# Gated attention and a maxout layer on one core: the product of the scores with v as seven half-block products in place of eight

## The chip, the core and the metric

The kernel runs on one core of a Trainium2 chip. Its time is the device time of one execution in microseconds, the median of several runs. TensorE (PE in the profile) does matrix products into PSUM, VectorE (DVE) and ScalarE (ACT) do elementwise work, GpSimd (POOL) issues the loads, and SyncE (SP) issues the transposing DMAs and the stores.

## What is computed

Eight sequences of 3072 rows. For each, with z of width 64 and u, v of width 256:

```python
scores = scale * np.matmul(z, z.transpose(0, 2, 1))     # scale = 1/3072
attn = np.maximum(scores, 0.0) ** 2
x = u * np.matmul(attn, v)                              # 24576 x 256 over all sequences
h1, h2 = x @ w1, x @ w2                                 # width 1024
out = np.maximum(h1, h2) @ w_out                        # 24576 x 256, float32
```

The kernel works in bfloat16 with float32 sums. It uses max(h1, h2) = relu(x (w1 - w2)) + h2, so that the second half of the layer is g w_out + x (w2 w_out), where the 256x256 product w2 w_out (`W2o_sb`) is made once.

## The kernel before

**Blocks.** A sequence is 24 blocks of 128 rows, and four blocks are a group, so there are six groups. One *step* makes one group of 512 output rows of the attention: 48 steps in all, `steps[n]` with `n = 6 b + s`. A step needs the squared scores of all 24 key blocks against its 512 rows.

**Scores.** z z^T is symmetric, so only the blocks on and above the diagonal are made (`scores_pair` for two key blocks by 512 rows, `scores_diag` for a group against itself). TensorE writes a pair into a PSUM tile of two banks (`s_ps`), ScalarE takes the relu into SBUF (`r_sb`, L218), VectorE squares it (`a_sb`, L221). Blocks above the diagonal are also turned by a transposing DMA into `aT` tiles, which a later step reads. The groups that a step reads turned are its `early` groups, the others are its own. Only in the first sequence are the first four groups made in both forms without turning.

**Products with v.** For each key block k and each half dc of v's columns, `attn` gives one matmul: 128x128 of v as weights, 128x512 of squared scores as the moving operand, summed in PSUM over the 24 blocks in `xacc0` and `xacc1`, one bank each. That is 48 matmuls of 512 columns per step. `epilogue` (L268) multiplies by u and scale on VectorE and gives `xT`.

**The layer.** `chunk_d` makes x (w1 - w2) in four pieces of 4 matmuls of 512 columns; each piece's relu goes to ScalarE or VectorE, whichever the scheduler finds free (`nc.any`, L292). `chunk_o` makes the output in two pieces of 20 matmuls of 256 columns, copied by ScalarE (L323) and stored.

**Order.** All matmuls, loads and SP's DMAs are pinned to program order. A list `work` holds the pieces of TensorE's work with a planned duration: products, d pieces (864 ns), o pieces (2180 ns). Steps are staggered, so that the d and o pieces of steps two and three back (`LAG = 3`) lie between the products of this step. Scores are made in *windows* of up to three pairs, which are laid into `work` from the last to the first, each as late as its rows are due (`LAT_OWN` and the like before use) and at least `GAP` apart, and not close to a d or o piece. VectorE's and ScalarE's instructions are placed by the scheduler by priority; `high_priority` puts some ahead. PSUM has eight banks: three tiles of two banks (`mm_psum`) are shared by scores, d and o pieces, two banks hold the sums of the products.

Of the kernel before, what the change touches and what calls it, by code (L numbers as in the profile page):

```python
# [11 lines left out]
def kernel(  # L12
# [31 lines left out]
    GW = G * P  # L44
    NG = NSB // G
# [5 lines left out]
    NA, NT, ND = 18, 12, 3  # L51
# [6 lines left out]
    vpool = ctx.enter_context(tc.tile_pool(name="vpool", bufs=2))  # L58
    ulpool = ctx.enter_context(tc.tile_pool(name="ulpool", bufs=3))
    upool = ctx.enter_context(tc.tile_pool(name="upool", bufs=3))  # L60
    xpool = ctx.enter_context(tc.tile_pool(name="xpool", bufs=LAG + 2))
    apool = ctx.enter_context(tc.tile_pool(name="apool", bufs=NA))
    dpool = ctx.enter_context(tc.tile_pool(name="dpool", bufs=ND))
    tpool = ctx.enter_context(tc.tile_pool(name="tpool", bufs=NT))
    gpool = ctx.enter_context(tc.tile_pool(name="gpool", bufs=2))
# [5 lines left out]
    pin = tc.keep_in_program_order  # L71

# [30 lines left out]
    def new_v():  # L103
        return vpool.tile([P, NSB, D], bf16, name="v_sb")

    def load_v(b, v_sb, t0, n):
        load(
            out=v_sb[:, ds(t0, n), :],
            in_=v[b].rearrange("(p t) d -> p t d", p=P)[:, ds(t0, n), :],
        )  # L110
# [40 lines left out]
    for q in seqs:  # L151
        q.T = {}
        q.u_sb = {}
        q.uT = {}

    w1_sb = consts.tile([P, KD, Dff], bf16)
    w2_sb = consts.tile([P, KD, Dff], bf16)
    w_out_sb = consts.tile([P, KF, D], bf16)
    w2T_sb = consts.tile([P, KD, KF, P], bf16)
    W2o_sb = consts.tile([P, KD, D], bf16)  # L160

    def subtract_weights():
        pin(nc.vector.tensor_sub(w1_sb, w1_sb, w2_sb))

    def turn_w2():
        sp_dma(
            out=w2T_sb.rearrange("p c n q -> p (c n) q"),
            in_=w2_sb.rearrange("p c f -> p (c f)"),
            transpose=True,
        )  # L170

    def fold_w2o():
        for dc in range(KD):
            w2o_ps = mm_psum.tile([P, D], fp32, name="w2o_ps", tag="mm")
            for nb in range(KF):
                matmul(
                    w2o_ps,
                    w2T_sb[:, dc, nb, :],
                    w_out_sb[:, nb, :],
                    start=(nb == 0),  # L180
                    stop=(nb == KF - 1),
                )
            nc.any.tensor_copy(W2o_sb[:, dc, :], w2o_ps)

# [17 lines left out]


    def scores_pair(b, s, k0):
        q = seqs[b]
# [4 lines left out]
        a_sb = apool.tile([P, 2, GW], bf16, name="a_sb")  # L210
        r_sb = apool.tile([P, 2, GW], bf16, name="r_sb", bufs=3)

        head = b == 0 and s == 0 and k0 < 12
        keep = pin if head else lambda ins: None
        if head and k0 in (2, 10):
            keep(nc.vector.tensor_single_scalar(out=r_sb, in_=s_ps, scalar=0.0, op=ALU.max))
        else:
            keep(nc.scalar.activation(r_sb, s_ps, AF.Relu))  # L218
        if head:
            yield  # L220
        keep(nc.vector.tensor_mul(a_sb, r_sb, r_sb))  # L221
        gj = k0 // G
        if gj > s and not direct(b, s, gj):
            if (s, gj) not in q.T:
                q.T[s, gj] = tpool.tile([P, G, G, P], bf16, name="aT")
            turn(
                q.T[s, gj][:, ds(k0 - G * gj, 2), :, :].rearrange("p k q x -> p (k q) x"),
                a_sb.rearrange("p j q -> p (j q)"),
            )
        yield a_sb  # L230
# [3 lines left out]
    def scores_diag(b, s):  # L234
        q = seqs[b]
        k = G * s
        s_ps = mm_psum.tile([P, 2 * G, P], fp32, name="s_ps", tag="mm")
        s2_ps = mm_psum.tile([P, 2 * G, P], fp32, name="s2_ps", tag="mm")
        score(q, s_ps[:, 0:4, :], 0, k, s, 0, 4)
        score(q, s_ps[:, 4:7, :], 1, k + 1, s, 1, 3)  # L240
        score(q, s2_ps[:, 2:4, :], 1, k + 2, s, 2, 2)
        score(q, s2_ps[:, 4:5, :], 0, k + 3, s, 3, 1)
        yield
        aD = dpool.tile([P, G, G, P], bf16, name="aD")
        r_sb = apool.tile([P, 7, P], bf16, name="r_sb", bufs=3)
        nc.scalar.activation(r_sb, s_ps[:, 0:7, :], AF.Relu)  # L246
        r2_sb = apool.tile([P, 3, P], bf16, name="r2_sb", bufs=2)
        nc.vector.tensor_single_scalar(out=r2_sb, in_=s2_ps[:, 2:5, :], scalar=0.0, op=ALU.max)  # L248
        nc.vector.tensor_mul(aD[:, 0, :, :], r_sb[:, 0:4, :], r_sb[:, 0:4, :])
        nc.vector.tensor_mul(aD[:, 1, 1:4, :], r_sb[:, 4:7, :], r_sb[:, 4:7, :])  # L250
        nc.vector.tensor_mul(aD[:, 2, 2:4, :], r2_sb[:, 0:2, :], r2_sb[:, 0:2, :])
        nc.vector.tensor_mul(aD[:, 3, 3, :], r2_sb[:, 2, :], r2_sb[:, 2, :])
        for r in range(G - 1):
            turn(
                aD[:, r + 1 : G, r, :],
                aD[:, r, r + 1 : G, :].rearrange("p q x -> p (q x)"),
            )
        yield aD

    def attn(q, k, moving, xacc, dcs, first, last):  # L260
        for dc in dcs:
            matmul(xacc[dc], q.v[:, k, ts(dc, P)], moving, start=first, stop=last)

    def epilogue(q, s, xacc):
        xT = xpool.tile([P, KD, GW], bf16, name="xT")
        with tc.high_priority(offset=2000):
            for dc in range(KD):
                nc.vector.scalar_tensor_tensor(  # L268
                    out=xT[:, dc, :].rearrange("p (t q) -> p t q", q=P),
                    in0=xacc[dc].rearrange("p (t q) -> p t q", q=P),  # L270
                    scalar=c2,
                    in1=q.uT[s][:, :, dc, :],
# [6 lines left out]
    def chunk_d(xT, g_out):  # L279
        g_sb = gpool.tile([P, KF, GW], bf16, name="g_sb")  # L280
        for nb in range(0, KF, 2):
            d_ps = mm_psum.tile([P, 2, GW], fp32, name="d_ps", tag="mm")
            for j in range(2):
                for kc in range(KD):
# [3 lines left out]
                        xT[:, kc, :],  # L288
# [3 lines left out]
            nc.any.tensor_single_scalar(  # L292
                out=g_sb[:, nb : nb + 2, :], in_=d_ps, scalar=0.0, op=ALU.max
            )
# [5 lines left out]
    def chunk_o(b, c, xT, g_sb, split=False):  # L300
        o_sb = opool.tile([P, G, D], fp32, name="o_sb")
        out_b = out[ds(b * S, S), :].rearrange("(p t) d -> p t d", p=P)
        def block(o_ps, t):
            for nb in range(KF):
                matmul(o_ps, g_sb[:, nb, ts(t, P)], w_out_sb[:, nb, :], start=(nb == 0), stop=False)
            for dc in range(KD):
                matmul(
                    o_ps, xT[:, dc, ts(t, P)], W2o_sb[:, dc, :], start=False, stop=(dc == KD - 1)
                )

        for th in range(G // 2):
# [7 lines left out]
            else:  # L319
# [3 lines left out]
                nc.any.tensor_copy(o_sb[:, ds(2 * th, 2), :], o_ps[:, :, :D])  # L323
# [8 lines left out]
    blank = consts.tile([P, GW], bf16)  # L332
# [12 lines left out]
    q.v = new_v()  # L345
    for t0 in range(0, NSB, G):
        load_v(0, q.v, t0, G)
# [6 lines left out]
    class Step:  # L354
        def __init__(self, b, s):
            self.b, self.s, self.q = b, s, seqs[b]
            self.xacc = None
            self.n = [0] * KD
# [7 lines left out]
            self.scored = {}  # L366

        def begin(self):


            self.xacc = [
                acc_psum.tile([P, GW], fp32, name=f"xacc{dc}") for dc in range(KD)
            ]

        def add(self, k, moving, dcs=range(KD)):
            n = self.n[dcs[0]]
            for dc in dcs:
                self.n[dc] += 1
            attn(self.q, k, moving, self.xacc, dcs, n == 0, n == NSB - 1)

        def add_early(self, k):
            i, qb = divmod(k, G)
            self.add(k, self.q.T[i, self.s][:, :, qb, :])

        def add_own(self, k, dcs=range(KD)):
            self.add(k, self.scored[k - k % 2][:, k % 2, :], dcs)
# [5 lines left out]
        def add_diag(self, j):  # L392
            self.add(G * self.s + j, self.scored[None][:, j, :, :])

        def finish(self):
            assert self.n == [NSB] * KD
            self.xT = epilogue(self.q, self.s, self.xacc)
            fresh[0] = self.xT[:, 0, 0:1]
# [14 lines left out]

    steps = [Step(b, s) for b in range(B) for s in range(NG)]

# [4 lines left out]
    LAT_OWN, LAT_TURNED, LAT_DIAG = 2900, 9000, 10000  # L420
# [3 lines left out]

    def put_early(st, ks):
# [274 lines left out]
```

## Time and profile before

| | |
|---|---|
| time, 3 runs | 981.18, 981.86, 981.88 us; median 981.86 |
| span of the profiled execution (its own time is known only as this span) | 979.7 us |
| TensorE busy, granted clock | 968.9 us (99%), 1.00 |
| VectorE busy | 432.0 us (44%) |
| ScalarE busy | 442.4 us (45%) |
| mean busy share of the DMA engines, by queue | 61.3% (hardware), 21.5% (software) |

The span is the time from the first to the last instruction; the time of a run is some 2 us more. "L74" is line 74 of the kernel; all matmuls have that line, so they are told apart by their tiles. A matmul's duration in the profile includes the time in the array's pipeline; what a stream of them costs is the distance between their starts. The same holds, with a smaller overlap, for VectorE and ScalarE.

### The profile page before, as it was taken

What the parts mean: (1) busy time and instruction counts of PE and PEld (TensorE: products, weight loads), DVE (VectorE), ACT (ScalarE), POOL (GpSimd) and SP (SyncE); (2) the same over time, 40 slices, a digit from 0 to 9 for tenths busy, and PEclk for the clock granted to TensorE, in tenths of its full rate; (3) what the DMA queues carried; (4) which work ended last, traced back from release to release, by engine and by line L of the source; (5) the groups of instructions that cost most, each with busy time, mean ns of one, the idle gap of its engine ahead of it and who ended that gap; (6) DMA issues with size and microseconds to landing.
All of it is one profiled execution on the core that took longest, in us unless ns stands there. A gap on an engine that the chain in (4) does not pass through costs nothing.

```text
span 979.7 us, 14514 instructions
## 1 busy us (share of the span) xinstructions
PE 968.9 (99%) x5661; PEld 510.6 (52%) x5742; DVE 432.0 (44%) x681; ACT 442.4 (45%) x500; POOL 77.5 (8%) x228
## 2 busy tenths in 40 slices
PE   9999999999999999999999999999999999999998
PEld 3355545555455554555545564455545555445556
DVE  6654444443544435433445334444345443554322
ACT  6853454334643355433554335533355433654322
POOL 2011100110001100010000100011000110000000
PEclk9999999999999999999999999999999999999999
DMA  9988899986989979898788968789777896896521
GB/s 150 186 142 150 145 180 153 165 147 114 182 161 149 150 118 180 152 168 130 150 157 144 175 122 164 142 153 181 135 147 149 135 188 126 148 164 115 109 66 65
DMA packets 378517, 143.46 MB, mean 146 GB/s; under 512 B 356944, under 2 KB 358608, under 8 KB 378448
## 3 DMA queue, kind: packets, MB, share of 16 engines
q1 hardware_dynamic: 361888, 112.78, 61.3%
q0 software_dynamic: 16560, 29.74, 21.5%
q8 instruction: 45, 0.74, 0.3%
q14 instruction: 24, 0.20, 0.1%
HBM read 59.77 MB, written 25.17 MB: 87 GB/s over the span
## 4 chain that ended last, share of the span: by engine, by line
PE 99%; issue 1%; DMA 0%; DVE 0%
PE xacc L74 52%; PE o_ps L74 21%; PE d_ps L74 17%; PE s_ps L74 8%; DMA o_sb<-in_z_dram 0%; PE tpz L134 0%; PE w2o_ps L74 0%; DVE o_sb L317 0%; DVE z_sb L343 0%
## 5 line engine op out<-in xcount | busy, mean ns | idle before, releaser
L74 PEld LDWEIGHTS <-v_sb 128*128 128x128 bf16 x2304 | 216.0, 98 | 277.4 <-issue 40.5
L218 ACT ACTIVATE r_sb<-s_ps 128x1024 bf16<-128x1024 f32 x258 | 248.5, 1023 | 111.4 <-PE s_ps L74 111.4
L221 DVE TENSOR_TENSOR a_sb<-r_sb 128x1024 bf16<-128x1024 bf16 x260 | 179.3, 691 | 212.1 <-ACT r_sb L218 207.9
L74 PE MATMUL xacc<-a_sb,v_sb 128*128 128x512 bf16 x997 | 231.0, 379 | 2.3 <-issue 0.2
L74 PE MATMUL xacc<-aT,v_sb 128*128 128x512 bf16 x912 | 216.5, 379 | 0.0
L74 PE MATMUL o_ps<-w_out_sb,g_sb 128*128 128x256 bf16 x1536 | 199.1, 273 | 0.0
L74 PE MATMUL d_ps<-xT,w_sb 128*128 128x512 bf16 x751 | 172.7, 379 | 0.9
L74 PEld LDWEIGHTS <-g_sb 128*128 128x128 bf16 x1536 | 149.9, 98 | 27.6
L292 ACT ACTIVATE g_sb<-d_ps 128x1024 bf16<-128x1024 f32 x96 | 98.3, 1024 | 138.8 <-PE d_ps L74 138.8
L292 DVE TENSOR_SCALAR g_sb<-d_ps 128x1024 bf16<-128x1024 f32 x96 | 117.4, 1223 | 84.7 <-PE d_ps L74 81.3
L323 ACT COPY o_sb<-o_ps 128x512 f32<-128x512 f32 x94 | 55.1, 586 | 178.2 <-PE o_ps L74 178.2
L268 DVE SCALAR_TENSOR_TENSOR xT<-xacc,uT 128x512 bf16<-128x512 f32 x96 | 62.0, 683 | 137.4 <-PE xacc L74 137.4
L74 PEld LDWEIGHTS <-w_sb 128*128 128x128 bf16 x768 | 75.1, 98 | 88.7
L74 PE MATMUL s_ps<-zT 64*128 64x512 bf16 (+3 forms) x696 | 89.2, 359 | 0.1
L246 ACT ACTIVATE r_sb<-s_ps 128x896 bf16<-128x896 f32 x44 | 40.3, 917 | 97.9 <-PE s_ps L74 97.9
L74 PE MATMUL xacc<-aD,v_sb 128*128 128x512 bf16 x331 | 79.9, 379 | 2.6 <-issue 2.2
L74 PE MATMUL o_ps<-W2o_sb,xT 128*128 128x256 bf16 x384 | 73.3, 273 | 0.0
L248 DVE TENSOR_SCALAR r_sb<-s_ps 128x384 bf16<-128x384 f32 x44 | 24.5, 558 | 95.3 <-PE s_ps L74 95.3
L74 PEld LDWEIGHTS <-zT 64*128 64x128 bf16 x696 | 27.2, 94 | 62.2 <-issue 50.4
L83 POOL COPY gate_sb<-g_sb 128x1 bf16<-128x1 bf16 x44 | 8.3, 188 | 420.0 <-DVE g_sb L292 253.2
L74 PEld LDWEIGHTS <-xT 128*128 128x128 bf16 x384 | 37.6, 98 | 4.4
L83 POOL COPY gate_sb<-a_sb 128x1 bf16<-128x1 bf16 x48 | 9.7, 203 | 273.9 <-DVE a_sb L221 273.9
(37 smaller groups left out, 144.2 us busy)
## 6 DMA issues: line engine op xcount, KB each, us to landing
out_dram<-o_sb SPq DMA_DIRECT2D x47, 512.0 KB, 3.7
v_sb<-in_v_dram POOLq DMA_DIRECT2D x48, 256.0 KB, 5.7
u_sb<-in_u_dram POOLq DMA_DIRECT2D x48, 256.0 KB, 5.3
aT<-a_sb SPq DMA_TRANSPOSE x228, 3.7
z_sb<-in_z_dram POOLq DMA_DIRECT2D x7, 384.0 KB, 7.5
aD<-aD SPq DMA_TRANSPOSE x132, 2.4
w_sb<-in_moe_w_dram POOLq DMA_DIRECT2D x2, 512.0 KB, 6.5
uT<-u_sb SPq DMA_TRANSPOSE x48, 4.8
```

Of the source, the lines that this page charges most:

```text
L74: pin(nc.tensor.matmul(*args, **kw))
L83: pin(nc.gpsimd.tensor_copy(gate_sb, tile_ap))
L218: keep(nc.scalar.activation(r_sb, s_ps, AF.Relu))
L221: keep(nc.vector.tensor_mul(a_sb, r_sb, r_sb))
L246: nc.scalar.activation(r_sb, s_ps[:, 0:7, :], AF.Relu)
L248: nc.vector.tensor_single_scalar(out=r2_sb, in_=s2_ps[:, 2:5, :], scalar=0.0, op=ALU.max)
L268: nc.vector.scalar_tensor_tensor(out=xT[:, dc, :].rearrange("p (t q) -> p t q", q=P), in0=xacc[dc].rearrange("p (t q) -> p t q", q=P), sca ...
L292: nc.any.tensor_single_scalar(out=g_sb[:, nb : nb + 2, :], in_=d_ps, scalar=0.0, op=ALU.max)
L323: nc.any.tensor_copy(o_sb[:, ds(2 * th, 2), :], o_ps[:, :, :D])
```

## The change

The products of a step from n = 4 on (`PLAIN = 4`; 44 of 48 steps) are made by a seven-product scheme of the Strassen kind. A product of a 2x2 arrangement of half blocks (two key blocks by two halves of v's columns, with two halves of 256 rows) takes seven matmuls of 256 columns in place of eight. They come in two phases:

- Phase 0: three products for each pair of key blocks, with *sums* of score half blocks (`make_sums`, two VectorE additions per group, into a buffer `es`) as moving operands, and sums of blocks of v (`lf`) as weights. Their three accumulators are copied to SBUF (`finish_sums`: one ScalarE copy of 768 columns, two VectorE additions).
- Phase 1: four products for each pair with score blocks as they are or with differences made in place (`make_split`, two VectorE subtractions per group). `finish` copies all four accumulators to SBUF on ScalarE and combines and scales them on VectorE (three float32 operations of 512 columns, four products with u of 256 columns).

The sums of v are made once per sequence and group (`fold_v`, five VectorE operations). The relus of the d pieces and the copies of the o pieces all go to ScalarE; so do four of five squares of the steps from n = 4 on (`square`). The squares are in place, so `r_sb` is gone. The diagonal group is made as a full pair and a lower quarter: two relus on ScalarE, two squares on VectorE, two turning DMAs in place of three. Phase 0 follows the o pieces of step n - 3; the d pieces of step n - 2 lie between the phases. Buffers: v and the score tiles are held by groups, `ulpool` 2 for 3, `xpool` 4 for 5, `gpool` 1 for 2; the two accumulators are one tile.

The core of the diff ("..." marks what is left out):

```diff
+    PLAIN = 4
-    NA, NT, ND = 18, 12, 3
+    NA, NT = 12, 12
+    vpool = ctx.enter_context(tc.tile_pool(name="vpool", bufs=10))
+    spool = ctx.enter_context(tc.tile_pool(name="spool", bufs=4))
+    epool = ctx.enter_context(tc.tile_pool(name="epool", bufs=1))
+    gpool = ctx.enter_context(tc.tile_pool(name="gpool", bufs=1))
...
+    def soon():
+        return tc.high_priority(offset=2000)
...
+    def fold_v(b, g):
+        q = seqs[b]
+        m = q.v[g].rearrange("p (m k) (c d) -> p m k c d", k=2, c=2)
+        lf = q.lf[g] = lpool.tile([P, 3, G // 2, P], bf16, name="lf")
+        sub, add = nc.vector.tensor_sub, nc.vector.tensor_add
+        add(lf[:, 0], m[:, :, 0, 0, :], m[:, :, 1, 1, :])
+        sub(lf[:, 1], m[:, :, 0, 1, :], m[:, :, 0, 0, :])
+        sub(lf[:, 2], m[:, :, 1, 0, :], m[:, :, 1, 1, :])
+        add(m[:, :, 0, 1, :], m[:, :, 0, 1, :], m[:, :, 1, 1, :])
+        add(m[:, :, 1, 0, :], m[:, :, 1, 0, :], m[:, :, 0, 0, :])
...
+    def square(ap):
+        n_squares[0] += 1
+        if n_squares[0] % 5:
+            nc.scalar.activation(ap, ap, AF.Square)
+        else:
+            nc.vector.tensor_mul(ap, ap, ap)
...
-            nc.any.tensor_single_scalar(
-                out=g_sb[:, nb : nb + 2, :], in_=d_ps, scalar=0.0, op=ALU.max
-            )
+            with soon():
+                nc.scalar.activation(g_sb[:, nb : nb + 2, :], d_ps, AF.Relu)
...
+        def make_sums(self, g):
+            es = spool.tile([P, 3 * GW], bf16, name="es")
...
+                a = self.A[g]
+                rows = es[:, : 2 * GW].rearrange("p (r x) -> p r x", x=HW)
+                nc.vector.tensor_add(rows, a[:, :, 0:HW], a[:, :, HW:GW])
+                cross = es[:, 2 * GW :].rearrange("p (m x) -> p m x", x=HW)
+                t = a.rearrange("p (m k) x -> p m k x", k=2)
+                nc.vector.tensor_add(cross, t[:, :, 0, 0:HW], t[:, :, 1, HW:GW])
...
+        def make_split(self, g):
...
+            nc.vector.tensor_sub(l1, l1, l0)
+            nc.vector.tensor_sub(h0, h0, h1)
...
+        def products(self, g, m, which):
...
+            if which == 0:
...
+                todo = [
+                    (0, lf[:, 2, m, :], rows[:, 2 * m + 1]),
+                    (1, lf[:, 1, m, :], rows[:, 2 * m]),
+                    (2, lf[:, 0, m, :], cross[:, m]),
+                ]
+            else:
+                todo = [
+                    (0, vk[:, 1, ts(1, P)], part[:, 1, 0]),
+                    (1, vk[:, 1, ts(0, P)], part[:, 1, 1]),
+                    (2, vk[:, 0, ts(1, P)], part[:, 0, 0]),
+                    (3, vk[:, 0, ts(0, P)], part[:, 0, 1]),
+                ]
...
+        def finish_sums(self):
+            e = epool.tile([P, 4, HW], fp32, name="e")
...
+                nc.scalar.copy(
+                    e[:, 0:3, :], self.acc.rearrange("p c (h x) -> p (c h) x", h=2)[:, 0:3, :]
+                )
+                self.w = epool.tile([P, 2, HW], fp32, name="w")
+                for h in range(2):
+                    nc.vector.tensor_add(self.w[:, h, :], e[:, h, :], e[:, 2, :])
...
+                nc.scalar.copy(e, self.acc.rearrange("p c (h x) -> p (c h) x", h=2))
+                nc.vector.tensor_add(t1, e[:, 0:2, :], e[:, 2:4, :])
+                nc.vector.tensor_add(w, w, e[:, 0:4:3, :])
+                nc.vector.tensor_sub(w, w, e[:, 1:3, :])
+                for h in range(2):
+                    for dc in range(KD):
+                        nc.vector.scalar_tensor_tensor(
...
-    LAT_OWN, LAT_TURNED, LAT_DIAG = 2900, 9000, 10000
+    LAT_OWN, LAT_TURNED, LAT_DIAG = 6500, 11500, 11500
+    AHEAD = 4500
...
+        if not st.plain:
+            put_o(n - LAG)
+            for which, ns in ((0, 327), (1, 437)):
+                if which:
+                    put(0, False, st.finish_sums)
+                    put_d(n - LAG + 1)
+                put(0, False, st.begin, () if which else "begin")
+                for g in st.groups:
+                    jobs.append((len(work), st, g, which))
...
-    for n in range(last - LAG + 2, last + 1):
-        put_d(n)
-        put_o(n - 1, False)
-    put_o(last, True)
+    put_o(last - LAG + 1)
+    for n in range(last - LAG + 2, last + 1):
+        put_d(n)
+        put_o(n, n == last)
...
-    GAP_FIRST, GAP = 2100, 2500
+    GAP_FIRST, GAP = 2100, 2400
...
-                v_at = [(3, 2), (3, 8), (3, 14), (4, 2), (4, 8), (4, 14)]
+                v_at = [(3, 8), (4, 2), (4, 8), (4, 13), (5, 9.5), (5, 11)]
...
+    waiting = sorted((begins[i] - AHEAD, i, st.n, g, which) for i, st, g, which in jobs)
...
+            elif which:
+                st.make_split(g)
+            else:
+                st.make_sums(g)
```

Sums and differences of a group are put into the program 4500 ns (`AHEAD`, by the planned durations) before the products that read them.

## The prediction

> **What bounds the kernel now.** First the page's busy times and its chain of waits:
>
> ```profile
> PE 968.9 (99%) x5661; PEld 510.6 (52%) x5742; DVE 432.0 (44%) x681; ACT 442.4 (45%) x500; POOL 77.5 (8%) x228
> PE 99%; issue 1%; DMA 0%; DVE 0%
> PE xacc L74 52%; PE o_ps L74 21%; PE d_ps L74 17%; PE s_ps L74 8%; DMA o_sb<-in_z_dram 0%; PE tpz L134 0%; PE w2o_ps L74 0%; DVE o_sb L317 0%; DVE z_sb L343 0%
> ```
>
> The chain is TensorE from end to end, and half of it is products with v. The table of waits shows 2.4 us for matmuls of the products and less for the others. So work taken from TensorE shortens the kernel, as long as the two engines at 45% can carry what is added. Then the groups by shape, for the price of one of each:
>
> ```profile
> L221 DVE TENSOR_TENSOR a_sb<-r_sb 128x1024 bf16<-128x1024 bf16 x260 | 179.3, 691 | 212.1 <-ACT r_sb L218 207.9 <-DMA aD<-aD 0.2
> L292 DVE TENSOR_SCALAR g_sb<-d_ps 128x1024 bf16<-128x1024 f32 x96 | 117.4, 1223 | 84.7 <-PE d_ps L74 81.3 <-issue 0.7
> L292 ACT ACTIVATE g_sb<-d_ps 128x1024 bf16<-128x1024 f32 x96 | 98.3, 1024 | 138.8 <-PE d_ps L74 138.8
> L268 DVE SCALAR_TENSOR_TENSOR xT<-xacc,uT 128x512 bf16<-128x512 f32 x96 | 62.0, 683 | 137.4 <-PE xacc L74 137.4
> L323 ACT COPY o_sb<-o_ps 128x512 f32<-128x512 f32 x94 | 55.1, 586 | 178.2 <-PE o_ps L74 178.2
> L251 DVE TENSOR_TENSOR aD<-r_sb 128x256 bf16<-128x256 bf16 x44 | 12.8, 291 | 1.5
> ```
>
> The figure after the busy time is the mean duration in ns. Durations overlap, so the timeline gives the spacing (start, length, and how many in the piece):
>
> ```profile
> 400.30 1.90 PE L74 MATMUL xacc<-aT,v_sb 128*128 128x512 bf16 x8
> 402.03 1.04 PE L74 MATMUL o_ps<-w_out_sb,g_sb 128*128 128x256 bf16 x8
> ```
>
> ```profile
> 399.88 2.85 ACT L218 ACTIVATE r_sb<-s_ps 128x1024 bf16<-128x1024 f32 x3 [1.03 <-PE s_ps L74]
> 413.92 0.43 DVE L249 TENSOR_TENSOR aD<-r_sb 128x512 bf16<-128x512 bf16 x1
> 414.26 0.35 DVE L250 TENSOR_TENSOR aD<-r_sb 128x384 bf16<-128x384 bf16 x1
> 414.83 0.69 DVE L221 TENSOR_TENSOR a_sb<-r_sb 128x1024 bf16<-128x1024 bf16 x1
> 415.44 1.28 DVE L268 SCALAR_TENSOR_TENSOR xT<-xacc,uT 128x512 bf16<-128x512 f32 x2
> ```
>
> A 512-column matmul costs (1.90 - 0.38)/7 = 0.216 us, one of 256 columns with weights of its own (1.04 - 0.27)/7 = 0.109. ScalarE: (2.85 - 1.02)/2 = 0.91 for 1024 columns. VectorE: 0.61 for a bf16 pair operation of 1024 columns, 0.34 for 512, 0.60 for 512 float32 columns. Each is about 0.09 to 0.11 below its duration.
>
> **TensorE, part by part.** Removed in 44 steps: 48 x 0.216 = 10.37 us. Added: six groups x two pairs of blocks x seven matmuls = 84 x 0.109 = 9.16. The o piece is the witness for 84: small matmuls, each with a new weight load, back to back. Gain 44 x 1.21 = 53.3 us. Turned tiles as moving operands come in four pieces of 128 columns today and cost no more than the others. The diagonal's scores grow from 10 blocks to 12; two 64-row matmuls run beside each other, so it is half a 256-column matmul, some 0.05 us x 44 = 2.2 us. One accumulator tile for two: in the plain steps 1 to 3 the next products wait for both L268 instructions (0.68 each) where now the first half's is over early, 3 x 0.9 = 2.7 us. The last o pieces now stand directly behind their own d pieces and wait for the last relu (about 0.5 us, twice): 1 us.
>
> A full step on TensorE is then 9.16 + d 16 x 0.216 = 3.46 + o 40 x 0.109 = 4.36 + scores 1.6 (8% of the span over 48 steps) = 18.6 us.
>
> **ScalarE per step.** 212 pairs fall into 44 steps, 4.82 each. Relus 4.82 x 0.91 = 4.4; squares 0.8 x 4.82 = 3.86, and no row shows a square there: between 0.91 (this relu) and 1.04 (its whole duration), I take 0.94, since a cast of 256 columns from SBUF (L344, 405 ns) is 0.03 over a copy of 256 from PSUM (L317, 372); 3.6. Diagonal 0.91 + 0.48 = 1.4. Accumulator copies 0.70 + 0.91 = 1.6. All d relus 4 x 0.91 = 3.6, o copies 2 x 0.48 = 1.0. Sum 15.6 us of 18.6, 84%.
>
> By the Trainium skill's page "ScalarE: Activation LUTs", Rules for kernel authors, relus and products belong on VectorE. The trace disagrees for the relus out of PSUM (1024 ns against VectorE's 1223) and bears it out for squares (0.61 on VectorE); with all squares back there VectorE's sum below would be 18.6 us per step, TensorE's own figure, and the forecast would go towards rival 1.
>
> **VectorE per step.** Sums 6 x (0.61 + 0.34) = 5.7; differences 6 x 2 x 0.34 = 4.1; `finish_sums` 2 x 0.34 = 0.7; `finish` 3 x 0.60 + 4 x 0.33 = 3.1; diagonal squares 0.61 + 0.34 = 0.95; its fifth of the squares 0.6; `fold_v` 5 x 0.21 = 1.05. Sum 16.2 us, 87%. From the other side, with whole durations (41 instructions x 0.09 more) it is 19.9. I take 16.2: the rows above overlap even where each follows the other at once.
>
> **Waits.** All of this is off the path only while it comes in time.
> - Between the phases TensorE has the d pieces (3.46) and after phase 1 the o pieces (4.36), ScalarE needs 0.70 and 0.91 for the accumulators: hidden, unless ScalarE is 2.5 us late.
> - d pieces come every 0.86 us and leave ScalarE every 0.91, with three PSUM tiles. If a score window stands right behind them, its third pair waits some 0.2 us for a tile.
> - Sums for phase 0: `finish` holds VectorE for 3.1 us out of the 8.2 us of o pieces and phase 0, in which the six sums need 5.7. That doesn't fit by 0.6, but four `es` buffers let VectorE make the first sums before, out of the 13% that it is free. What can't be made before are rows scored late. The tightest window of own rows stands 1.75 us before phase 1's end (the planner keeps 1.7 us to the next o piece). Three relus, the accumulator copy, the rest of the window before and three squares end about 8.6 us later, the sum at 9.6; TensorE gets there at 1.75 + 0.87 (scores) + 4.36 + four groups x 0.65 = 9.6. So about 0, and 0.3 for the diagonal behind it.
> - Loads: `v_at` puts the last two of a sequence behind the last reader of an old group; POOL's queue waits there, the u load behind it too, and a `fold_v` that VectorE has in its order can hold up everything on it, 0 to 2 us at seven seams; 4 us in all.
>
> I take 0.3 us per step, 13 us, with bounds of 0 and 0.8 (35 us). SP has fewer DMAs (88 diagonal turns for 132), the other turns are the same.
>
> **Sum.** Against the span: 979.7 - 53.3 + 2.2 + 2.7 + 1 + 13 + 4 = 949.3. The median of the runs is 2.2 over the span: 951.5, say 951. Without any wait 979.7 - 53.3 + 2.2 + 2.2 = 930.8; with 35 us of waits and 14 at the seams 983.
>
> **Rivals.**
> 1. *VectorE becomes the bound* (slower). Place: sums, differences and `finish` on one in-order queue. If nothing overlaps, 19.9 us per step: 44 x 1.3 = 57 us over TensorE's floor of 935 (the sum without waits at steps and seams), 992. It decides from 19.8 us per step on (53.3 - 5.9 = 47.4 us to lose, 1.1 per step). For: 87% with two queues that wait for each other, and stretches where ScalarE has three windows in a step. Against: the overlaps. Chance 0.26.
> 2. *Strided operands lose the double rate* (slower). No bf16 pair operation of the trace has pieces of 128 or 256 columns with gaps. If these ran at a column per cycle (L292 on VectorE, 1.14 spacing), sums and differences would be 17.6 instead of 9.8, VectorE 24 us per step, some 1170 us. The Trainium skill, "VectorE: DVE Perf Modes", Mode 2×_1P, asks for 16-bit data of step 1 only, which these have; the trace shows that rate on whole tiles (691 ns). Chance 0.04.
> 3. *Relu and square don't share a table* (slower). The one table load in the trace takes 1.28 us; two per window, 2.3 windows per step, make 5.9 us more on ScalarE: 21.5 per step, about 1065. The Trainium skill, "ScalarE: Activation LUTs", Table sets, names relu and copy as in every set, not square. Chance 0.03.
> 4. *The transfers come too late*: turned tiles and v with the DMA engines at 83% already. Turns take 3.7 us to land and are planned 11.5 ahead; a delay of 1.2 us per step would take the gain. About 990. Chance 0.05.
>
> **Numbers.** TensorE stays the bound: 0.62, its own range 931 to 983. Rival 1 reaches from 970 to 1010 and has a little of "faster". A measurement here tells about 0.2% (2 us) from no change. Faster 0.66, same 0.03, slower 0.31. The range leaves out rivals 2 and 3 and the top of 1: 931 to 1008.
>
> **What would show it.** TensorE's busy time near 920 us; 256-column products 0.109 apart; VectorE and ScalarE each some 740 us of spacing (more in durations); TensorE's waits named `es` (sums), not `acc`. Wrong it is if products wait for VectorE over 1.1 us per step, if small matmuls are over 0.115 apart, or if bf16 sums of 1024 columns take more than 0.7 us.

## The result, and the profile after

The changed kernel takes 1108.28 us (median of four runs, 1104.19 to 1109.73), the kernel before 981.56 beside it: a ratio of 1.1286, 95% interval 1.1265 to 1.1306. It is 12.9% slower; the forecast was 951, faster. The profiled execution took 1108.47 us, with a span of 1106.7 and a mean granted clock of 0.951 (1.000 before).

Busy times, granted clock in 40 slices, and chain, from the page of the changed kernel:

```profile
PE 990.1 (89%) x7326; PEld 678.2 (61%) x7326; DVE 763.8 (69%) x1887; ACT 779.0 (70%) x898; POOL 221.6 (20%) x228
...
PEclk8889978999899998999989999899998999989999
...
PE 47%; ACT 20%; DMA 14%; DVE 11%; issue 7%; POOL 1%; SPq 0%; DVEq 0%; ACTq 0%; POOLq 0%
PE acc L81 24%; PE o_ps L81 10%; PE d_ps L81 9%; DMA v_sb<-in_v_dram 7%; ACT g_sb L323 7%; ACT a_sb L249 6%; DMA aT<-a_sb 6%; ACT a_sb L230 4%; PE s_ps L81 4%; DVE es L462 2%; DVE xT L544 1%; DVE a_sb L253 1%; ACT a_sb L284 1%; ACT e L519 1%; DVE es L465 1%
```

No engine is busy over 89%, and the chain, TensorE from end to end before, is less than half TensorE. Two transfers stand in it: the load of v (7%) and the turning DMAs (6%). From the sixth slice on the clock dips every five slices, about once per sequence. The groups (busy time, mean ns of one; behind the second bar the idle time ahead of them and what ended it):

```profile
L81 PE MATMUL acc<-es,lf 128*128 128x256 bf16 x1584 | 217.7, 286 | 87.7 <-DVE lf L203 52.6
...
L230 ACT ACTIVATE a_sb<-a_sb 128x1024 bf16<-128x1024 bf16 x170 | 183.6, 1102 | 0.9
...
L90 POOL COPY gate_sb<-g_sb 128x1 bf16<-128x1 bf16 x43 | 60.5, 1408 | 487.3 <-ACT g_sb L323 487.3
L462 DVE TENSOR_TENSOR es<-a_sb 128x1024 bf16<-128x1024 bf16 x150 | 102.9, 686 | 39.1 <-ACT a_sb L230 35.3
...
L483 DVE TENSOR_TENSOR a_sb<-a_sb 128x512 bf16<-128x512 bf16 x150 | 63.0, 420 | 61.0 <-DMA aT<-a_sb 60.9
...
L201 DVE TENSOR_TENSOR lf<-v_sb 128x256 bf16<-128x256 bf16 x48 | 13.8, 288 | 104.3 <-DMA v_sb<-in_v_dram 104.3
```

The instructions cost what the forecast said: sums of 1024 columns 686 ns, pieces with gaps 420 ns for 512, squares on ScalarE 1102 ns, and 256-column products 0.110 us apart where nothing holds them (the first line of the timeline below: (2.79 - 0.27)/23). What is new stands behind the second bar: VectorE is idle 104.3 us ahead of the first fold of v and 60.9 us ahead of the differences, and the seven-product matmuls of phase 0 (`acc<-es,lf`) stand 87.7 us. The waits say the same by pairs (us in total, times, longest):

```profile
DVE lf L201 <- DMA v_sb<-in_v_dram: 104.3, 24, 5.9
...
DVE a_sb L483 <- DMA aT<-a_sb: 60.9, 35, 4.0
...
PE acc L81 <- DVE lf L203: 52.6, 15, 9.0
...
ACT e L519 <- DVE a_sb L484: 45.5, 9, 6.6
...
PE acc L81 <- DVE es L462: 34.5, 26, 3.5
PE acc L81 <- DVE xT L298: 10.6, 3, 4.0
```

VectorE waits for v at three or four places of each sequence; one of them lies at the seam, where one sequence goes over into the next, and there TensorE stops too. One seam in the timeline (start, length; in brackets the idle time before and its releaser), from TensorE's, GpSimd's and VectorE's rows:

```profile
414.43 2.79 PE L81 MATMUL acc<-aT,v_sb 128*128 128x256 bf16 x24
...
423.93 3.33 POOL L90 COPY gate_sb<-a_sb 128x1 bf16<-128x1 bf16 x1 [11.45 <-ACT a_sb L230]
427.20 0.53 POOL L93 DMA_DIRECT2D v_sb<-in_v_dram  x1
...
426.53 0.68 DVE L462 TENSOR_TENSOR es<-a_sb 128x1024 bf16<-128x1024 bf16 x1
431.77 0.29 DVE L201 TENSOR_TENSOR lf<-v_sb 128x256 bf16<-128x256 bf16 x1 [4.56 <-DMA v_sb<-in_v_dram]
...
432.79 0.42 DVE L465 TENSOR_TENSOR es<-a_sb 128x512 bf16<-128x512 bf16 x1
...
432.53 1.46 PE L81 MATMUL acc<-es,lf 128*128 128x256 bf16 x6 [5.41 <-DVE lf L203]
434.81 2.74 PE L81 MATMUL acc<-es,lf 128*128 128x256 bf16 x12 [0.82 <-DVE lf L203]
```

Four things are to be seen. The load of v is issued at 427.20, behind a one-column copy of GpSimd (`gate`, which holds a load until a given tile is written) that took 3.33 us; it ended when VectorE's gapless stream of two-input instructions ended (426.53 + 0.68). Before, such a copy took 0.2 us (from the groups of before):

```profile
L83 POOL COPY gate_sb<-a_sb 128x1 bf16<-128x1 bf16 x48 | 9.7, 203 | 273.9 <-DVE a_sb L221 273.9
```

The fold that needs this load is VectorE's next instruction: everything behind it on that queue stands for 4.56 us, among it a score sum (L465) whose blocks were there, since the sum at 426.53 reads the same ones. TensorE then stands 5.41 us. And when it goes on, twelve small matmuls take 2.74 us, 0.22 us each where they took 0.11: half clock.

Adding up the distances between the starts of matmuls, less the usual distance of their kind, TensorE's standstills of over 0.3 us are 131.6 us in 88 places (7.3 us before): 57.5 inside phase 0, 38.9 at the seven seams (4.4 to 6.8 each, between a score window and phase 0). The granted clock is 0.5 in 16 stretches, some 109 us together.

### The profile page after: what moved, and what is told of

It reads as the page before. It is cut to its first block, busy times and chain, and to the rows that moved or that the text cites. A ratio compares the mean times of both kernels' runs of the same rounds, so it can differ in the third digit from the quotient of the medians.

```text
span 1106.7 us, 19307 instructions
## 1 busy us (share of the span) xinstructions
PE 990.1 (89%) x7326; PEld 678.2 (61%) x7326; DVE 763.8 (69%) x1887; ACT 779.0 (70%) x898; POOL 221.6 (20%) x228
## 4 chain that ended last, share of the span: by engine, by line
PE 47%; ACT 20%; DMA 14%; DVE 11%; issue 7%; POOL 1%; SPq 0%; DVEq 0%; ACTq 0%; POOLq 0%
PE acc L81 24%; PE o_ps L81 10%; PE d_ps L81 9%; DMA v_sb<-in_v_dram 7%; ACT g_sb L323 7%; ACT a_sb L249 6%; DMA aT<-a_sb 6%; ACT a_sb L230 4%; PE s_ps L81 4%; DVE es L462 2%; DVE xT L544 1%; DVE a_sb L253 1%; ACT a_sb L284 1%; ACT e L519 1%; DVE es L465 1%
## 5 line engine op out<-in xcount | busy, mean ns | idle before, releaser
L81 PE MATMUL acc<-es,lf 128*128 128x256 bf16 x1584 | 217.7, 286 | 87.7 <-DVE lf L203 52.6
L249 ACT ACTIVATE a_sb<-s_ps 128x1024 bf16<-128x1024 f32 x258 | 251.0, 1039 | 56.8 <-PE s_ps L81 56.3
L81 PEld LDWEIGHTS <-lf 128*128 128x128 bf16 x1584 | 159.0, 102 | 139.3 <-DVE lf L203 60.1
L81 PE MATMUL acc<-a_sb,v_sb 128*128 128x256 bf16 (+1 forms) x1392 | 195.9, 293 | 10.6 <-DVE xT L298 10.6
L323 ACT ACTIVATE g_sb<-d_ps 128x1024 bf16<-128x1024 f32 x192 | 181.8, 1033 | 16.2 <-PE d_ps L81 14.2
L230 ACT ACTIVATE a_sb<-a_sb 128x1024 bf16<-128x1024 bf16 x170 | 183.6, 1102 | 0.9
L90 POOL COPY gate_sb<-g_sb 128x1 bf16<-128x1 bf16 x43 | 60.5, 1408 | 487.3 <-ACT g_sb L323 487.3
L462 DVE TENSOR_TENSOR es<-a_sb 128x1024 bf16<-128x1024 bf16 x150 | 102.9, 686 | 39.1 <-ACT a_sb L230 35.3
L81 PE MATMUL acc<-aT,v_sb 128*128 128x256 bf16 x912 | 111.7, 273 | 0.0
L81 PE MATMUL s_ps<-zT 64*128 64x512 bf16 (+1 forms) x696 | 101.4, 374 | 9.2 <-ACT g_sb L323 2.2
L483 DVE TENSOR_TENSOR a_sb<-a_sb 128x512 bf16<-128x512 bf16 x150 | 63.0, 420 | 61.0 <-DMA aT<-a_sb 60.9
L452 DVE TENSOR_TENSOR es<-aT 128x1024 bf16<-128x1024 bf16 x114 | 78.1, 685 | 12.0 <-DMA aT<-a_sb 10.8
L201 DVE TENSOR_TENSOR lf<-v_sb 128x256 bf16<-128x256 bf16 x48 | 13.8, 288 | 104.3 <-DMA v_sb<-in_v_dram 104.3
L90 POOL COPY gate_sb<-a_sb 128x1 bf16<-128x1 bf16 x41 | 44.2, 1078 | 207.4 <-ACT a_sb L230 143.6
```

The source lines that it names most:

```text
L81: pin(nc.tensor.matmul(*args, **kw))
L90: pin(nc.gpsimd.tensor_copy(gate_sb, tile_ap))
L201: add(lf[:, 0], m[:, :, 0, 0, :], m[:, :, 1, 1, :])
L230: nc.scalar.activation(ap, ap, AF.Square)
L249: keep(nc.scalar.activation(a_sb, s_ps, AF.Relu))
L323: nc.scalar.activation(g_sb[:, nb : nb + 2, :], d_ps, AF.Relu)
```

## The experiments

Four explanations: **v**, the loads of v and the folds behind them hold up VectorE's queue at the seams; **turns**, the differences are made in place and must wait until the turning DMA has read the tile; **amount**, VectorE (rival 1) or ScalarE has too much to do; **clock**, the standstills cost more than their length, since TensorE is slower behind them. The ratios are to the kernel before on the same chip, with 95% intervals. `e2` to `e5`, `e10` and `e11` leave work out and so don't compute the whole result; the others do.

**One cause taken away at a time.**

`e1_no_gate`: `- if is_load:` becomes `+ if is_load and begins[i] < start_of[0, 4]:` ahead of `gate(...)`, so that loads after the first steps aren't held by GpSimd copies.

> The loads from the fifth step of the first sequence on have no GpSimd copy ahead of them any more; they wait only for their buffers. Theory A (the sums of v stand in VectorE's queue and wait for v; v is late because the copy ahead of each load reads SBUF and waits for a gap in VectorE's stream, 1.1 to 4.2 us in the mean in place of 0.2): VectorE's wait for v falls from 104 us to under 40, the time from 1108 to 1030 to 1060. Theory B (v is late because its buffer comes free late): the wait stays over 80 us, time over 1090. Theory C (VectorE simply has too much to do, rival 1 of the prediction): time within 1% of 1108.

1104.19 us, 1.1251 [1.1201, 1.1302]. The time is the one named for **amount** and not the one named for the copies (theory A). But the waits moved: VectorE's wait for v fell from 104.3 to 48.5 us, and its wait for turns rose from 60.9:

```profile
DVE a_sb L483 <- DMA aT<-a_sb: 117.8, 43, 7.6
```

What the loads gave back, the next DMA on the same queue took.

`e2_v_once`: the loads and folds of later sequences are left out, and the first sequence's v serves for all. In their place stands

```diff
+            seqs[c].v, seqs[c].lf = seqs[0].v, seqs[0].lf
```

> v and its sums are loaded and made once and used for all sequences (leaves out the other seven sequences' v and its sums). Theory A: all waits of TensorE for sums of v (7 gaps, 39 us) and VectorE's 104 us for v go, with them some of the gaps for score sums and of the half-clock stretches: 1010 to 1040. Theory C: only the work counts, 1.05 us per step of VectorE: 1060 to 1108. If differences waiting for the turning DMAs were most of it (theory D): over 1070.

1022.95 us, 1.0424 [1.039, 1.0457]: 85 us less, though the 210 folds left out are, at 0.21 us, only 44 us of VectorE, and v's loads are DMAs. The clock rose to 0.985. The wait for turns was now 102.5 us.

`e3_no_war`: the differences of groups that are not read turned go to a tile of their own that nothing reads, so that VectorE does the same work and need not wait for the turning DMA.

```diff
-            nc.vector.tensor_sub(l1, l1, l0)
-            nc.vector.tensor_sub(h0, h0, h1)
+            if g in self.early:
...
+            else:
+                d = spool.tile([P, 3 * GW], bf16, name="es")
+                for i, (x, y) in enumerate(((l1, l0), (h0, h1))):
...
```

> The differences of a step's own groups go to a scratch tile that nothing reads, so that VectorE does the same work but need not wait until the turning DMA has read the scores (leaves out those differences). Theory D (this wait, 61 us of VectorE's idle time, holds up the score sums behind it): 1040 to 1075. Theory A alone: 1095 to 1108. Theory C: within 1% of 1108.

1069.27 us, 1.0896 [1.0864, 1.0927]: 39 us less, with the same arithmetic. v's wait stayed at 101.0.

`e4_no_sums`: no sums and no differences at all, the same number of matmuls on raw blocks.

> No score sums and no differences: the products read the score blocks as they are (leaves out make_sums and make_split, 9.8 us of VectorE per step; the same 84 matmuls). The floor of the prediction is 935. If waits for VectorE are the whole loss: 940 to 985, the rest being the wait for sums of v at seven places (39 us and its clock). If ScalarE can't keep up with relus and squares: over 1020, with TensorE waiting for ScalarE.

1016.44 us, 1.0357 [1.0285, 1.0429], between the two ranges. 92 us of the loss go, and with the differences the wait for turns goes too, so this alone does not tell amount from turns. But **amount** can't be all: VectorE is busy only 342 us, and the kernel is still slower than before, with 138.1 us of VectorE's waits for v. The GpSimd copies are short again here:

```profile
L90 POOL COPY gate_sb<-g_sb 128x1 bf16<-128x1 bf16 x43 | 8.5, 197 | 482.8 <-ACT g_sb L323 464.6 <-DMA a_sb<-a_sb 18.2
```

So the length of the copies isn't what makes v late, or not alone: with short ones, too, a fold stands on VectorE until its load has landed (at one seam a load issued at 381.78 us lands at 388.2, and VectorE waits 5.8 us for it).

`e5_v_once_no_war`: `e2` and `e3` together.

> Both earlier edits together: v and its sums once for all sequences, and own groups' differences into a scratch tile (leaves both out). Theory A+D (the two DMA waits in VectorE's queue, with the half-clock stretches that they cause, are the loss): the single gains were 85 and 39 us of 1108, so 975 to 990, and the granted clock over 0.99. Theory C (VectorE's amount of work): not under 1010.

988.44 us, 1.0076 [1.0048, 1.0103], clock 0.993. Its busy line:

```profile
PE 951.2 (97%) x7326; PEld 669.5 (68%) x7326; DVE 720.3 (73%) x1677; ACT 777.2 (79%) x898; POOL 237.6 (24%) x144
```

VectorE carries 94% of the changed kernel's work and ScalarE all of it, and 120 of the 127 us of loss are gone. The two waits for DMAs, with what hangs on them, were the loss, not the sums; **amount** is out as its cause.

**Order by hand.** The scheduler is free to place VectorE's instructions. It puts some ahead of their plan: in the trace after, score sums of step 4 stand in the plain steps and wait 4.58 us for a turn there, ahead of an `epilogue`.

`e6_pinned`: folds, sums and differences all held in program order (`pin(...)` around each). `e7_pinned_early_v`: also v loaded earlier:

```diff
-    NA, NT = 12, 12
+    NA, NT = 11, 12
...
-    vpool = ctx.enter_context(tc.tile_pool(name="vpool", bufs=10))
+    vpool = ctx.enter_context(tc.tile_pool(name="vpool", bufs=12))
...
-                v_at = [(3, 8), (4, 2), (4, 8), (4, 13), (5, 9.5), (5, 11)]
+                v_at = [(3, 8), (4, 2), (4, 8), (4, 13), (5, 1), (5, 4)]
```

`e8_pinned_early_v_late_split`: also the differences placed 2.0 us ahead of their products, not 4.5.

> The whole computation; sums of v, score sums and differences are kept in program order on VectorE, in place of the order that the scheduler chose from its own guess of when DMAs land. Theory E (it is the order: instructions that wait for a DMA were floated ahead of work that was ready): 1030 to 1070, and the three waits of 3 to 4 us in the plain steps go. Theory A+D with the lateness in the data (loads and turns land too late whatever the order): 1095 to 1120.

> As the one before, and v's last two groups are loaded 8 and 7 us earlier into two more buffers (one score tile fewer pays for them), the whole computation. Theory A: VectorE's wait for v falls under 40 us and the time is 20 to 50 us under the run with pinned order alone. If v's loads are late because GpSimd's copy waits for VectorE and not because of the plan: under 15 us better.

> As the one before, and the differences are put 2.0 us ahead of their products in place of 4.5. Theory D: the wait for turning DMAs shrinks by half, 10 to 30 us better than the run before it; if then the differences come late for the products themselves, TensorE waits for them and it is slower than the run before it.

1137.91 us (1.1592 [1.1535, 1.1649]), 1086.0 (1.1063 [1.1031, 1.1095]) and 1104.39 (1.1251 [1.1218, 1.1283]). `e6` lies outside both of its ranges, and holding everything costs 30 us over the changed kernel. There TensorE still waits 45.0 us for folds, and the sums behind a late fold can't go ahead of it any more. `e7` is 52 us under `e6`: VectorE's wait for v is gone and the clock is 0.996. But products of phase 0 wait for sums some 50 times, 82 us, while ScalarE waits 135 us for VectorE and VectorE some 290 for ScalarE: I read it as a strict order across two queues that makes each wait for the other. In `e8` differences come late for their products, some 9 us in 17 places; the other half of its 18 us over `e7` is not explained.

**The whole computation, mended.** `e9_all_fixes`: early v as in `e7`, no `gate` for v's loads, all differences into `es` tiles, and sums held in order only while the plain steps run. `e13_own_diffs`: only the own groups' differences in tiles, the turned and diagonal groups' in place. `e14_own_diffs_5`: `e13` with five `es` buffers for four, one less for v and for `lf`, and v's last load 5 us later for it. `e15_own_diffs_sq3`: `e13` with a third of the squares on VectorE for a fifth.

> The whole computation, with what the runs so far point to: v's last groups loaded earlier into two more buffers (one score tile fewer), no GpSimd copy ahead of v's loads, the differences into tiles of the sums' pool in place of in place, and the first sums held in program order while the plain steps run. If the two DMA waits were the loss and nothing new comes up: near the run without v's reloads and without the wait for turns, 985 to 1000. If the four buffers that sums and differences now share make VectorE wait for TensorE: 1010 to 1060.

> The whole computation, as the run with all the fixes, but only the groups that a turning DMA reads (a step's own) get their differences in tiles of the sums' pool; the others are made in place again. If the shared four tiles held VectorE up (92 us of waits for products in that run): 985 to 1000. If not: 1005 to 1015.

> The same with five tiles in that pool, paid for with one v buffer and one buffer for sums of v. If tiles are still short: 5 to 15 us better than the run with four. If v's last group comes late again for want of its buffer: worse.

> As the first of these three, with a third of the squares on VectorE in place of a fifth. If ScalarE's emptying of PSUM is the larger part of what is left (23 us of TensorE waiting for PSUM tiles): up to 10 us better; if VectorE's queue is: worse by as much.

1011.31 us (1.0302 [1.0285, 1.032]), 1014.50 (1.0338 [1.0318, 1.0358]), 1011.22 (1.0303 [1.0287, 1.0318]) and 1005.61 (1.0255 [1.023, 1.028]). Some 97 us come back at once. Then where the differences go (`e13`) and a fifth `es` buffer (`e14`) change 3 us each, and a third of the squares on VectorE (`e15`) gives 9. `e15`'s timeline shows what is left, once per sequence (GpSimd's rows, then VectorE's):

```profile
195.47 3.17 POOL L90 COPY gate_sb<-g_sb 128x1 bf16<-128x1 bf16 x1 [11.66 <-ACT g_sb L328]
...
199.10 1.07 POOL L93 DMA_DIRECT2D v_sb<-in_v_dram  x2
...
204.44 0.29 DVE L201 TENSOR_TENSOR lf<-v_sb 128x256 bf16<-128x256 bf16 x1 [5.84 <-DMA v_sb<-in_v_dram]
```

The copy holds the load of u, and v's loads, which need no copy now, stand behind it in GpSimd's queue until 199.10. The fold waits at 198.6 already, though it is planned a step later: the scheduler had moved it ahead.

`e16_folds_held` is `e15` with the folds held in program order too, and `e17_folds_held_sq2` has half of the squares on VectorE. `e18_only_folds_held` is the opposite check: the changed kernel with only that edit.

```diff
-        sub, add = nc.vector.tensor_sub, nc.vector.tensor_add
+        def sub(*a):
+            pin(nc.vector.tensor_sub(*a))
+
+        def add(*a):
+            pin(nc.vector.tensor_add(*a))
```

> The whole computation, as the run with own differences and a third of the squares on VectorE, and the sums of v are held in program order on VectorE. In that run the scheduler had floated one of them a step ahead of its plan, in each sequence, to a place where v was still behind a u load's GpSimd copy: a wait of TensorE of 4.0 us each time, with half clock after it. If that is what was left: 7 x (4.0 + 1.5 to 3) = 38 to 49 us less than 1005.6, so 957 to 975, faster than the kernel before. If v is late wherever its sums stand: 995 to 1010.

> The same with half of the squares on VectorE. ScalarE is 0.13 x 4.8 x 0.94 = 0.8 us per step lighter by it than with a third, VectorE 0.5 us heavier by 0.17 x 4.8 x 0.61. If TensorE's waits for PSUM tiles (21 us) are still ScalarE's: 2 to 8 us faster than the other; if VectorE's queue is now the later one: slower.

> The changed kernel with one edit: the sums of v are held in program order on VectorE; loads, GpSimd's copies and in-place differences as they were. Theory A in its last form (the scheduler floats the sums of v ahead of their plan, to where v has not landed): VectorE's wait for v falls from 104 us to under 50, the seven long waits of TensorE for sums of v shrink, 1040 to 1075, and the wait for the turning DMAs stays. If v's loads are late also at the planned place (the copies ahead of them wait for VectorE, the last two wait for their buffers): 1085 to 1115.

971.39 us (nine runs, 971.05 to 983.25), 0.9914 [0.9888, 0.9939]; 968.87, 0.9871 [0.9858, 0.9884]; 1115.13, 1.1358 [1.1325, 1.1391]. The first two compute everything and are faster than both kernels, than the one before by 0.9 and 1.3%. Busy times, chain and two waits of `e17`:

```profile
PE 939.4 (97%) x7318; PEld 667.8 (69%) x7326; DVE 800.2 (83%) x1951; ACT 717.9 (74%) x834; POOL 181.1 (19%) x186
...
PE 78%; ACT 13%; issue 3%; DVE 1%; DVEq 0%; ACTq 0%
```

```profile
PE acc L81 <- DVE es L462: 4.6, 1, 4.6
...
PE acc L81 <- DVE lf L201: 3.4, 7, 0.5
```

VectorE has 36 us more to do than in the changed kernel, and the kernel is 139 us faster. ScalarE has 61 less, but that isn't it: `e15` and `e16` have the same load there (750 us) and lie 34 us apart. The chain, which the profile follows back over 95% of the span, has no DMA in it any more. `e18` came out the second way: the order alone gives nothing, since with v still late at its planned place TensorE waits 70.3 us for folds. So holding the folds pays once v is loaded early and the other mends are in. Which of these mends it needs besides early loads was not run.

**The floor.** `e10_v_once_no_sums`: `e2` and `e4` together. `e11_v_once_no_sums_sq_dve`: also all squares on VectorE (`if n_squares[0] % 5:` becomes `if False:`).

> v and its sums once, no score sums and no differences (leaves all of them out): 84 small matmuls per step with VectorE nearly idle. It measures the floor of the prediction, 935 with its small terms. Theory F (the matmuls' gain is as summed, and what is left above it comes from VectorE): 935 to 950. Theory G (ScalarE empties PSUM too late for TensorE, with relus, copies and four fifths of the squares): 955 to 985, TensorE waiting for ScalarE at scores and d pieces.

> The same with all squares on VectorE. Theory G: 10 to 30 us faster than the one before it. Theory F: within 5 us of it.

966.11 us, 0.9844 [0.9825, 0.9864], and 948.70, 0.9667 [0.9648, 0.9686]. With VectorE at 299 us `e10` still has 17 us that go when ScalarE is relieved. In starts of matmuls they are third score pairs (29 places, 13.6 us) and d pieces (14 places, 8.0 us) that wait for a PSUM tile which ScalarE has yet to empty; in `e11` 1.2 us are left. `e10`'s waits name the relus of the d pieces:

```profile
PE d_ps L81 <- ACT g_sb L323: 5.7, 14, 0.4
PE s_ps L81 <- ACT g_sb L323: 4.8, 15, 0.4
```

**The clock by itself.** `e12_before_with_gaps`: the kernel before with a wait at the head of each step, made of GpSimd copies in a row that one small matmul waits for. Sequences 1 and 2 have one copy, 4 and 5 twelve.

```diff
+            chain = {1: 1, 2: 1, 4: 12, 5: 12}.get(self.b, 0)
+            for i in range(chain):
+                pin(nc.gpsimd.tensor_copy(late_sb, late_sb if i else steps[n - 1].xT[:, 0, :P]))
+            if chain:
...
+                matmul(late_ps[:, :P], late_sb[:, :P], late_sb[:, :P], start=True, stop=True)
```

> The kernel before with a wait of TensorE put at the head of each step: one small GpSimd copy long (1.5 to 2.5 us) in sequences 1 and 2, twelve copies long (4 to 7 us) in sequences 4 and 5, none in the others. Theory H (waits of a few us halve the granted clock afterwards): in sequences 4 and 5 stretches of half clock, 3 us or more of them per wait, so that a step costs its wait and 2 us or more besides; in sequences 1 and 2 few or none. If the clock falls for another reason: full clock throughout, each step longer by its wait alone.

1093.93 us in one run. Two places of its timeline, and windows with short and long gaps (us, then busy time of PE, PEld, DVE, ACT, POOL with instructions, clock, DMA share, GB/s):

```profile
160.04 0.23 PE L74 MATMUL late_ps<-late_sb 128*128 128x128 bf16 x1 [1.52 <-POOL late_sb L373]
160.11 3.62 PE L74 MATMUL d_ps<-xT,w_sb 128*128 128x512 bf16 x16
...
526.90 0.29 PE L74 MATMUL late_ps<-late_sb 128*128 128x128 bf16 x1 [5.77 <-POOL late_sb L373]
526.98 6.42 PE L74 MATMUL d_ps<-xT,w_sb 128*128 128x512 bf16 x16
```

```profile
252.00:374.00 122.00, 115.59 (x672) 58.95 (x672) 49.10 (x79) 49.69 (x56) 10.09 (x31) 1.00 0.79 141
...
497.00:660.00 163.00, 131.26 (x697) 65.78 (x698) 50.46 (x82) 49.93 (x58) 31.14 (x100) 0.88 0.58 108
```

The same 16 matmuls take 3.62 us behind a short gap and 6.42 behind a long one. All twelve gaps of 0.9 to 1.5 us left the clock at 1.00; each of the twelve of 4.8 to 5.8 us was followed by 3.4 to 6.8 us at half clock. A sequence with long gaps takes 166.9 us against 120.2 without: 33.1 are the gaps, and 13.6, or 2.3 us for each, the clock. So **clock** holds, as a surcharge on long waits.

## Why the prediction was wrong, point by point

**TensorE's part** held in its main term. In `e11` the products take 469.6 us from start to start against 511.3, 41.7 less where 53.3 were forecast. Once the first sequence is over, six steps spend 56.5 us on products for 63.2, or 1.11 us less per step where the forecast had 1.21; that is 4 of the missing 11.6, and the rest lies in the first sequence. Scores take 8.4 us more (93.1 against 84.7), not 2.2: six steps spend 10.86 us on them for 10.14, or 5.3 in 44 steps, so that term was too small, and 2.5 are waits of the plain steps behind a score window, which the forecast had as a term of its own. o pieces take 1.7 more. The sum, 31.6, is within 0.1 us of the difference of the spans (979.7 and 948.0). So 31.7 us are there to be had with the sums, later loads of v and ScalarE's squares taken away.

**The engines' loads** held in amount. VectorE and ScalarE are busy 763.8 and 779.0 us in durations. Rival 2 is out (420 ns for 512 columns in pieces), rival 3 too (one table load in the whole trace). Rival 1, likeliest of the rivals, is out as told: `e17` gives VectorE more work and is fast. The profile's page had the sign that busy time wasn't the question: the chain named DMAs.

**The waits** are where it failed: the terms of 13 us for the steps and 4 for the seams. Even their upper bounds, 35 and 14, were passed three times over: 158.7 us lie between `e11`'s span and the changed kernel's, 3.6 per step, and 119 of them are standstills of over 0.3 us (131.6 less `e11`'s 12.3).

- *"Loads: ... 0 to 2 us at seven seams; 4 us in all."* The mechanism is named rightly there, even that a fold "can hold up everything on it". Its size was not worked out: the wait is the whole time from the issue to the landing of a load (4.57 us in the seam shown, 427.20 to 431.77), and the issue itself came late behind a GpSimd copy. Seven seams cost 38.9 us of standstill, and `e2` shows 85 us in all with what hangs on them. The prediction gave GpSimd's copies no price of their own: 188 to 203 ns on average before, 1.1 to 4.2 us after, by what they read. It saw GpSimd's queue wait, but for a free buffer, not behind a copy that VectorE's new stream slows. That slowing is no more than a part of it: in `e4` the copies take 0.2 to 0.6 us on average, and VectorE waits 138.1 us for v.
- *The differences in place.* The sum priced them as 0.34 us of VectorE each and asked what they need, not what still needs their tile. The row of the turning DMAs was there (3.7 us to land). VectorE waits 60.9 us for them, and without that wait (`e3`) the kernel is 39 us faster. This wait was on no list.
- *"One accumulator tile for two ... 3 x 0.9 = 2.7 us."* 10.6 us by the waits: sums of step 4 that the scheduler had put ahead of `epilogue` waited for their turns. 3.7 are left with the sums held in order there (`e17`) or gone (`e11`), near the forecast.
- *"d pieces ... three PSUM tiles ... some 0.2 us."* The mechanism was right and its size too small: 21.6 us in 43 places by starts in `e10`, 0.5 us each, and 17 us in the time.
- *Half clock* was no term at all. At 1.000 in every slice of before there was no row for it, yet a standstill of 5 us costs 7.3. In the changed kernel 40 us (158.7 less the 119) are no standstill; 32 of them are matmuls that run slower inside the half-clock stretches.

**Rival 4** (transfers too late) was the nearest, but it was thought of as a lack of DMA bandwidth. The DMA engines are less busy than before (71.5% by queues for 82.8). The transfers are late because of where they were issued and where their readers stood in a queue.

**Signs named beforehand.** "Products wait for VectorE over 1.1 us per step" came true (52.6 + 34.5 us are 2.0 per step) and rightly marked the failure; matmuls 0.109 apart and sums under 0.7 us came true as well. TensorE's waits named `es`, but `lf`, the sums of v, came first. The "busy time near 920 us" did not come: 990.1, and 933.5 at best (`e11`).

What stays open: the 20 us between `e17` and `e11`. Some 10 are third score pairs waiting for tiles (11.7 us against 1.2) and 9 phase 0 waiting for sums, of scores once (4.8) and of v seven times (0.65); no run takes these two apart with the whole computation.

## What to carry to other kernels

When work is moved to an engine that is half idle, list for each instruction of its in-order queue what DMA it reads and what DMA still reads the tile it overwrites: one such wait holds everything behind it, and the busy share doesn't show it. Load early, don't write in place onto data that a transfer still reads, and keep just those instructions that wait for a transfer at their planned place; holding everything in order is worse (`e6` took 30 us more than the changed kernel). Taking away one of two such waits can give nothing (`e1`, `e18`), so a miss doesn't clear a cause.

## What the runs showed of the hardware that was not expected

- TensorE's granted clock falls to 0.5 behind standstills of 4.8 to 5.8 us and not behind those of 0.9 to 1.5; 2.3 us for each. The Trainium skill, "TensorE: Matmul & The Clock Gate", Part 1, has the clock halved after an idle window of about 3.4 us and released after a busy one. The trace of `e12` agrees: stretches of 3.4 to 6.8 us. So does the changed kernel for its twelve waits of 3.2 us and more, which all have such a stretch; but five of its nine waits of 1.9 to 2.7 us have one too, which an idle window of 3.4 us doesn't explain. Why, no run here shows.
- A one-column copy on GpSimd took 188 to 203 ns before and 1408 (L90 from `g_sb`) after. VectorE's busy share doesn't set it: the same copies take 4669 ns in `e5`, where VectorE is 73% busy, 2638 in `e17` (83%), and 186 in `e10`, which has no sums and differences. In the seam shown it ended with VectorE's stream of two-input instructions. The Trainium skill, "SBUF — State Buffer", Who interferes with whom, says that a VectorE instruction with two SBUF inputs contends with a GpSimd instruction that reads SBUF. The trace agrees, and shows what follows for the loads queued behind such a copy.
- Bfloat16 additions on pieces of 128 or 256 columns with gaps run as fast as on whole rows (418 to 420 ns for 512 columns and 686 for 1024, against 425 and 691 before). Relu and square alternate on ScalarE with one table load in the whole trace.
